# Batch 0's last stages on the PSUM pools of the dense layers, and batch 1's first matmuls ahead of the first dense matmul

## The chip, the cores and the metric

One Trainium2 chip, one core. The metric is the device time of one execution in microseconds (us), without tracing. Every kernel here was run several times on the same chip as the kernel before, alternating with it; a profiled execution was taken beside those.

## The reference

A global filter (real FFT over 3008 positions, product with a learnt filter, inverse FFT) is followed by a two-layer network with an exact gelu:

```python
X = np.fft.rfft(x, axis=1)                      # x: 8 x 3008 x 256
y = np.fft.irfft(X * (filt_r + 1j * filt_i)[None], n=x.shape[1], axis=1)
h = y.reshape(8 * 3008, 256) @ w_in             # 256 x 2048
g = 0.5 * h * (1.0 + erf(h / np.sqrt(2.0)))
out = g @ w_out                                 # 2048 x 256, float32
```

## The kernel before

In this text an evacuation is the copy of a finished PSUM bank (where TensorE writes) into SBUF, a store goes from SBUF to DRAM, and a readback fetches what was stored.

Each transform is a two-stage DFT, 3008 = 47 x 64, written as matmuls with tables T1 to T4 that the kernel makes for itself. The program order is written by hand; a scheduler does not reorder it.

**The front** handles batch 0 alone. Its stages c1, c1t (transposes), c2 (with the filter product), c3, c3t (transposes) and c4 pass everything through SBUF, while the tables are made beside them:

```python
def dup_filters(self, eng, k0, k):           # filter rows 0..63 copied to rows 64..127
    for k in range(k0, k0 + k, 2):
        o, i = (self.F[r:r + 64, :, k:k + 2, :].rearrange("p t a b -> p t (a b)") for r in (64, 0))
        eng.tensor_copy(out=o, in_=i)

def table_3_turn(self, q):                   # T3i from T3, with the sign columns turn_r, turn_i
    k = slice(8 * q, 8 * q + 8)
    for r in range(2):
        self.nc.vector.tensor_scalar(out=self.T3i[:, k, r, :], in0=self.T3[:, k, 1 - r, :],
                                     scalar1=self.turn[r], scalar2=None, op0=ALU.mult)

def c4(self, u, eng):                        # last stage of batch 0: y
    d = self.st[0, "d", u // 2]
    for half in range(2):
        ps = self.bank("ps_c4", "v")
        for i in range(4):
            self.nc.tensor.matmul(ps[:, 94 * i:94 * i + 94], lhsT=d[...], rhs=T4c, ...)
        self._evac(yv, ps[...], eng[half], 1.0 / self.S)
```

```python
m.load_x(1)                                  # batch 1's x, 8 loads on the GpSimd queue
m.load_w_out(0)                              # second-layer weights, 2 loads behind them
m.load_w_out(8)
...
wide = ctx.enter_context(ExitStack())
m.psum(wide, v=(4, 1), t=(4, 1))             # eight PSUM banks for c3t and c4
for u in range(10):
    if u < 8:
        m.c3t(u)
    if u >= 2:
        m.c4(u - 2, (act, False if u > 7 else act))
wide.close()
m.psum(ctx, h=(3, 1), o=(2, 1), f=(3, 1))    # the eight banks of the steady part
```

**The steady part** is a sequence of slots. A slot has two first-layer matmuls (`mm1`, 128x512, gelu on ScalarE from a bank "h") and, from slot 16 on, four second-layer matmuls of the tile before (`mm2`, into a bank "o"). The transforms of the later batches are laid into slots. These pass through DRAM: stage 1 stores `a`, which is read back as `b`; stage 3 stores `v`, which is read back as `d`. Stage 1:

```python
self.pa = pool("pa", 3)                      # three a buffers
...
def s1(self, b, c):                          # four groups c = 0..3 for each batch
    a = self.pa.tile([128, 2, 4, 256], BF16, tag="a", name="a_sb")
    ps = [[self.bank("ps_s1", "h" if i == h == 0 else "f") for h in range(2)] for i in range(2)]
    ...                                      # eight matmuls from x
    for i in range(2):
        for h in range(2):                   # four evacuations by VectorE
            self._evac(a[:, h, 2 * i:2 * i + 2, :]..., ps[i][h], False)
    for r in range(2):
        for h in range(2):                   # four stores of 96 KB on the sync queue
            nc.sync.dma_start(out=o[:, w:w + 4, :], in_=a[64 * r:64 * r + 48, h])
```

```python
# batch 1: first slot and spacing of stage 1, slot of b's readback, stage 2 ... stage 4
s1, n1, r1, s2, n2, r2, s4, n4 = 1, 4, 16, 26, 2.8, 61, 68, 0.72
...
for s in range((NT + 1) * 16):
    t, jc = s // 16, s % 16
    for f, a in at.pop(s, ()):               # the stages laid into this slot come first
        f(*a)
    if t >= 1:
        m.mm2(t - 1, jc)
    if t < NT:
        m.mm1(t, jc)
```

So stage 1 of batch 1 stands in slots 1, 5, 9 and 13.

## Time and profile before

| | |
|---|---|
| time | 772.72 us, median of 3 runs (772.1 to 775.15) |
| profiled execution | span 770.6 us |
| TensorE busy | 99% of the span |
| last c4 matmul starts | 37.82 us |
| second pair of first-layer matmuls starts | 39.84 us |
| first second-layer matmul starts | 49.13 us |

The page, the seam, the front and the stage-4 wait are shown in the prediction. How to read such lines: PE is TensorE, PEld its weight loads, DVE VectorE, ACT ScalarE, POOL GpSimd and SPq the sync queue. A timeline line has the start and the length in us, the engine, the line of the program, the operation, output and inputs by name and shape, and how many instructions the line joins. The square bracket is idle time of that engine before the line and what the profile thinks ended it. L296 (before) and L300 (after) are stage 1; L482 and L486 the first dense layer; L509 and L513 the second; L271 and L275 VectorE's evacuations; L459 and L463 are c4.

DMA issues between 38 and 50 us (what, queue, count, KB each, median us from issue to landing):

```profile
R<-a_sb SPq DMA_DIRECT2D x14, 96.0 KB, 2.3
```

A store of stage 1 takes 2.3 us there in the median. The four stores of the first group took 3.1 to 3.7 us.

### The profile page before, as it was taken

How to read it: one execution, taken by the hardware profiler on the slowest of the kernel's cores; microseconds unless marked ns; L12 is line 12 of the kernel's file. 1: busy time of each engine (PE TensorE's matmuls, PEld its weight loads, DVE VectorE, ACT ScalarE, POOL GpSimd, SP SyncE). 2: the span in 40 equal slices, each digit the busy share in tenths (PEclk: the TensorE clock that was granted, in tenths of full speed). 3: DMA queues.
4: the chain of work that ended last, by engine and by line, in shares of the span. 5: the costliest groups of instructions: out<-in, count | busy, mean ns of one | idle time of the engine just before them, and what ended most of it. 6: DMA issues, size and time to landing. Idle time of an engine off the chain costs nothing.

```text
span 770.6 us, 15044 instructions
## 1 busy us (share of the span) xinstructions
PE 763.5 (99%) x6057; PEld 527.5 (68%) x6057; DVE 398.5 (52%) x737; ACT 566.7 (74%) x977; POOL 62.5 (8%) x154
## 2 busy tenths in 40 slices
PE   8999999999999999999999999999999999999998
PEld 5857666776766766677777777667676777766666
DVE  8957755564545645466463664627646366411011
ACT  6879855897568975699656996579865798666663
POOL 7701100010000200011000110001100000000000
PEclk9999999999999999999999999999999999999999
DMA  9884645366163661636526364345553422410111
GB/s 153 150 197 115 136 125 129 115 138 155 40 173 88 128 158 47 187 79 125 138 58 176 85 133 124 83 151 105 114 137 84 136 83 70 123 42 28 42 42 55
DMA packets 87270, 85.66 MB, mean 111 GB/s; under 512 B 6688, under 2 KB 77472, under 8 KB 87200
## 3 DMA queue, kind: packets, MB, share of 16 engines
q1 hardware_dynamic: 78816, 68.70, 31.3%
q0 software_dynamic: 8384, 16.00, 14.1%
q8 instruction: 47, 0.77, 0.4%
q14 instruction: 23, 0.19, 0.1%
HBM read 54.00 MB, written 46.66 MB: 131 GB/s over the span
## 4 chain that ended last, share of the span: by engine, by line
PE 94%; DMA 3%; POOL 2%; issue 0%; DVE 0%; POOLq 0%; SPq 0%
PE ps_o L509 43%; PE ps_h L482 42%; PE ps_s L369 2%; PE ps_s L344 2%; PE ps_s L319 2%; PE ps_s L296 2%; DMA x_sb<-in_x_dram 2%; POOL x_sb L83 1%; DMA F<-in_filt_i_dram 1%; POOL F L97 1%; DMA d_sb<-R 0%; POOL F L92 0%; PE ps_e L499 0%; POOL T1s L282 0%; DVE ost L522 0%
## 5 line engine op out<-in xcount | busy, mean ns | idle before, releaser
L485 ACT ACTIVATE g_sb<-ps_h 128x512 bf16<-128x512 f32 x752 | 438.0, 597 | 183.4 <-PE ps_h L482 172.6
L509 PE MATMUL ps_o<-w_out_sb,g_sb 128*128 128x256 bf16 x2992 | 447.5, 273 | 0.0
L482 PE MATMUL ps_h<-y_sb,w_in_sb 128*128 128x512 bf16 (+3 forms) x1600 | 445.8, 366 | 0.7 <-DMA x_sb<-in_x_dram 0.7
L509 PEld LDWEIGHTS <-g_sb 128*128 128x128 bf16 x2992 | 283.9, 98 | 134.3 <-issue 9.9
L482 PEld LDWEIGHTS <-w_in_sb 128*128 128x128 bf16 x1600 | 154.7, 98 | 23.7 <-issue 1.1
L515 DVE COPY ost<-ps_o 128x512 f32<-128x512 f32 x93 | 63.8, 686 | 143.5 <-PE ps_o L509 143.4
L327 DVE TENSOR_TENSOR p<-ps_s,F 128x512 bf16<-128x512 f32 x84 | 58.1, 692 | 105.8 <-ACT p L326 89.4
L273 DVE TENSOR_SCALAR y_sb<-ps_s 128x376 bf16<-128x376 f32 x112 | 61.0, 548 | 80.7 <-PE ps_s L369 80.7
L271 DVE CAST a_sb<-ps_s 128x512 bf16<-128x512 f32 x112 | 69.4, 683 | 27.7 <-PE ps_s L296 27.7
L271 DVE CAST v_sb<-ps_s 128x512 bf16<-128x512 f32 x84 | 57.4, 685 | 2.9 <-PE ps_s L344 2.9
L325 ACT ACTIVATE p<-ps_s 64x512 bf16<-64x512 f32 x84 | 49.8, 593 | 2.0
L326 ACT CAST p<-ps_s 64x512 bf16<-64x512 f32 x84 | 48.5, 577 | 1.0
L369 PEld LDWEIGHTS <-d_sb 96*128 96x128 bf16 x448 | 30.7, 97 | 25.6 <-DMA d_sb<-R 0.6
L102 POOL COPY gate<-p 1x1 bf16<-1x1 bf16 x48 | 8.5, 176 | 470.7 <-DVE p L329 470.7
L329 DVE TENSOR_TENSOR p<-p 128x512 bf16<-128x512 bf16 x84 | 35.7, 425 | 2.9
L369 PE MATMUL ps_s<-T,d_sb 96*128 96x94 bf16 x448 | 36.3, 204 | 0.1
L328 DVE TENSOR_TENSOR p<-p,F 128x512 bf16<-128x512 bf16 x84 | 34.9, 415 | 0.0
L83 POOL DMA_DIRECT2D x_sb<-in_x_dram x64 | 32.6, 511 | 13.3 <-issue 12.8
L344 PE MATMUL ps_s<-p,T 128*128 128x256 bf16 x168 | 32.1, 273 | 0.0
L319 PE MATMUL ps_s<-b_sb,T 128*128 128x256 bf16 x168 | 32.1, 273 | 0.0
L344 PEld LDWEIGHTS <-T 128*128 128x128 bf16 x168 | 16.4, 98 | 20.1 <-DVE p L329 0.5
L319 PEld LDWEIGHTS <-T 128*128 128x128 bf16 x168 | 16.4, 98 | 13.4
(113 smaller groups left out, 195.0 us busy)
## 6 DMA issues: line engine op xcount, KB each, us to landing
out_dram<-ost SPq DMA_DIRECT2D x93, 256.0 KB, 2.4
x_sb<-in_x_dram POOLq DMA_DIRECT2D x64, 188.0 KB, 3.6
R<-a_sb SPq DMA_DIRECT2D x112, 96.0 KB, 2.1
b_sb<-R SPq DMA_DIRECT2D x28, 384.0 KB, 4.1
R<-v_sb SPq DMA_DIRECT2D x42, 256.0 KB, 3.3
d_sb<-R SPq DMA_DIRECT2D x56, 192.0 KB, 4.7
w_in_sb<-in_moe_w_in_dram POOLq DMA_DIRECT2D x2, 512.0 KB, 9.0
w_out_sb<-in_moe_w_out_dram POOLq DMA_DIRECT2D x2, 512.0 KB, 11.0
```

Source lines behind the costliest of these rows:

```text
L271: self.nc.vector.tensor_copy(out=out, in_=in_)
L273: self.nc.vector.tensor_scalar(out=out, in0=in_, scalar1=scale, scalar2=None, op0=ALU.mult)
L319: nc.tensor.matmul(ps[:, 256 * i:256 * i + 256], lhsT=self.T2[:, k].rearrange("p a b -> p (a b)"), rhs=self.st[b, "b", k // 6][:, k % 6, : ...
L325: nc.scalar.activation(out=p2[0:64], in_=ps[64:128], func=AF.Copy, scale=-1.0)
L326: nc.scalar.copy(out=p2[64:128], in_=ps[0:64])
L327: nc.vector.tensor_tensor(out=p1, in0=ps, in1=f(0), op=ALU.mult)
L344: nc.tensor.matmul(ps[:, 256 * i:256 * i + 256], lhsT=self.T3[:, k].rearrange("p a b -> p (a b)"), rhs=w[:, 256 * i:256 * i + 256], start= ...
L369: nc.tensor.matmul(ps[:, 94 * i:94 * i + 94], lhsT=d[:, (grp % 2) * 4 + i, 128 * half:128 * half + 128], rhs=t4, start=True, stop=True)
L482: nc.tensor.matmul(ps[:, o:o + n], lhsT=self.w_in_sb[:, dc, jc * 128:jc * 128 + 128], rhs=self.ring[:, dc, off:off + n], start=(dc == 0), ...
L485: nc.scalar.activation(out=self.st["g", t][:, jc, :], in_=ps, func=AF.Gelu)
L509: nc.tensor.matmul(ps[:, tile_i % 2, :], lhsT=g[:, jc, tile_i * 128:tile_i * 128 + 128], rhs=self.w_out_sb[:, jc, :], start=(jc == 0), sto ...
L515: nc.vector.tensor_copy(out=ost, in_=ps)
```

## The change

The intent: VectorE's small table work early in the kernel is shortened (sign columns by memsets, one filter copy to ScalarE, other small work later), and the seam between batch 0's transform and the dense layers is closed. For that c3t and c4 use the banks of the steady part, so no pool is closed and reopened, and batch 1's first stage-1 group moves in front of the first dense matmul. The core of the diff, with cuts:

```diff
 def dup_filters(self, eng, k0, k):
-            eng.tensor_copy(out=o, in_=i)
+            (eng.copy if eng is self.nc.scalar else eng.tensor_copy)(out=o, in_=i)
 ...
-    def turn_signs(self, g):      # five VectorE operations on 128x1 columns
-        ts(out=q, in0=self.p, scalar1=64.0, scalar2=-64.0, op0=ALU.is_ge, op1=ALU.mult)
-        ...
+    def signs(self, g):           # eight memsets
+        for t, s in zip(self.turn, (-1.0, 1.0)):
+            set_(t, s)
+            for lo in (32, 96):
+                set_(t[lo:lo + 32], -s)
+        set_(self.wtc, 2.0)
+        set_(self.wtc[0:4], 1.0)
 ...                               # weights_4: VectorE -> GpSimd, after the w_out loads
 ...                               # table_2_rows earlier, T1c later
+    m.dup_filters(nc.scalar, 0, 2)
     m.table_3_copy(1, False)
-    m.dup_filters(nc.vector, 0, 4)
+    m.dup_filters(nc.vector, 2, 2)
 ...
-        ps = self.bank("ps_c3t", "t", BF16)
+        ps = self.bank("ps_c3t", "f", BF16)
 ...
-            ps = self.bank("ps_c4", "v")
+            ps = self.bank("ps_c4", "h" if (2 * u + half) % 5 < 3 else "o")
 ...
-    wide = ctx.enter_context(ExitStack())
-    m.psum(wide, v=(4, 1), t=(4, 1))
+    m.psum(ctx, h=(3, 1), o=(2, 1), f=(3, 1))
     for u in range(10):
         if u < 8:
             m.c3t(u)
         if u >= 2:
-            m.c4(u - 2, (act, False if u > 7 else act))
-    wide.close()
-    m.psum(ctx, h=(3, 1), o=(2, 1), f=(3, 1))
+            m.c4(u - 2, (False if u > 7 else act, act))
 ...
-            s1, n1, r1, s2, n2, r2, s4, n4 = 1, 4, 16, 26, 2.8, 61, 68, 0.72
+            s1, n1, r1, s2, n2, r2, s4, n4 = 0, 4, 15, 25, 2.8, 61, 68, 0.72
```

Stage 1 of batch 1 now stands in slots 0, 4, 8 and 12.

More of the change, by code (lines that the diff above doesn't have):

```diff
@@ L137, in table_1 @@
         ts(out=hc, in0=h, scalar1=-2.0 * PI, scalar2=2.0 * PI, op0=ALU.mult, op1=ALU.add)
-        self.turn_signs(g)
-        self.weights_4(g)
+        self.table_2_rows(g)
         w, r = g.tile([128, 2, K1], FP32, name="w1"), g.tile([128, 2, K1], FP32, name="r1")
@@ L177, in table_2_angle @@
                                    in1=jn.unsqueeze(1).to_broadcast([128, 6, NB]), op0=ALU.mult, op1=ALU.add)
+            self.T1c = g.tile([2 * NA, 96], BF16, name="T1c")
+            v.tensor_copy(out=self.T1c.rearrange("p (k h r) -> p k h r", h=2, r=2),
+                          in_=self.T1.rearrange("p (h r k) -> p k h r", h=2, r=2))
             ts(out=w[:, 6:12], in0=w[:, 0:6], scalar1=n6, scalar2=None, op0=ALU.add)
@@ L183, in table_2_angle, with weights_4 @@
            op0=ALU.logical_shift_left)
-    def turn_signs(self, g):
-        ts = self.nc.vector.tensor_scalar
-        q, b = (g.tile([128, 1], FP32, name=n) for n in ("q64", "b32"))
+    def signs(self, g):
+        set_ = self.nc.vector.memset
         self.turn = [g.tile([128, 1], FP32, name=n) for n in ("turn_r", "turn_i")]
-        ts(out=q, in0=self.p, scalar1=64.0, scalar2=-64.0, op0=ALU.is_ge, op1=ALU.mult)
-        self.nc.vector.tensor_tensor(out=q, in0=self.p, in1=q, op=ALU.add)
-        ts(out=b, in0=q, scalar1=32.0, scalar2=2.0, op0=ALU.is_ge, op1=ALU.mult)
-        ts(out=self.turn[0], in0=b, scalar1=1.0, scalar2=-1.0, op0=ALU.mult, op1=ALU.add)
-        ts(out=self.turn[1], in0=b, scalar1=-1.0, scalar2=1.0, op0=ALU.mult, op1=ALU.add)
+        for t, s in zip(self.turn, (-1.0, 1.0)):
+            set_(t, s)
+            for lo in (32, 96):
+                set_(t[lo:lo + 32], -s)
+        self.wtc = g.tile([128, 1], FP32, name="wtc")
+        set_(self.wtc, 2.0)
+        set_(self.wtc[0:4], 1.0)
+    def weights_4(self, g):
+        ts = self.nc.gpsimd.tensor_scalar
+        q, self.wt = (g.tile([128, 1], FP32, name=n) for n in ("q48", "wt"))
+        ts(out=q, in0=self.p, scalar1=48.0, scalar2=-48.0, op0=ALU.is_ge, op1=ALU.mult)
+        self.nc.gpsimd.tensor_tensor(out=q, in0=self.p, in1=q, op=ALU.add)
+        ts(out=self.wt, in0=q, scalar1=2.0, scalar2=1.0, op0=ALU.is_ge, op1=ALU.add)
     def unit_matrices(self, g, cols):
@@ L218, in table_2_swap @@
                        "act", 1.0 - 2.0 * i)
-    def weights_4(self, g):
-        ts = self.nc.vector.tensor_scalar
-        q, self.wt, self.wtc = (g.tile([128, 1], FP32, name=n) for n in ("q48", "wt", "wtc"))
-        ts(out=q, in0=self.p, scalar1=48.0, scalar2=-48.0, op0=ALU.is_ge, op1=ALU.mult)
-        self.nc.vector.tensor_tensor(out=q, in0=self.p, in1=q, op=ALU.add)
-        ts(out=self.wt, in0=q, scalar1=2.0, scalar2=1.0, op0=ALU.is_ge, op1=ALU.add)
-        ts(out=self.wtc, in0=self.p, scalar1=4.0, scalar2=1.0, op0=ALU.is_ge, op1=ALU.add)
     def table_4(self, t4, t1, wt, tag, eng):
@@ L562 @@
     m.warm_up(10)
+    m.signs(g)
     m.table_1(g)
-    m.table_2_rows(g)
-    m.T1c = g.tile([2 * NA, 96], BF16, name="T1c")
-    nc.vector.tensor_copy(out=m.T1c.rearrange("p (k h r) -> p k h r", h=2, r=2),
-                          in_=m.T1.rearrange("p (h r k) -> p k h r", h=2, r=2))
     m.gen = m.py.tile([128, 2, K1, NB], FP32, tag="y", name="gen")
@@ L637 @@
     m.load_w_out(8)
+    m.weights_4(g)
     warm = g.tile([128, 1], FP32, name="warm")
```

## The prediction

> **What bounds the kernel now.** I read the page first, for the shares and the chain that ended last.
>
> ```profile
> PE 763.5 (99%) x6057; PEld 527.5 (68%) x6057; DVE 398.5 (52%) x737; ACT 566.7 (74%) x977; POOL 62.5 (8%) x154
> PE ps_o L509 43%; PE ps_h L482 42%; PE ps_s L369 2%; PE ps_s L344 2%; PE ps_s L319 2%; PE ps_s L296 2%; DMA x_sb<-in_x_dram 2%; POOL x_sb L83 1%; DMA F<-in_filt_i_dram 1%; POOL F L97 1%; DMA d_sb<-R 0%; POOL F L92 0%; PE ps_e L499 0%; POOL T1s L282 0%; DVE ost L522 0%
> ```
>
> TensorE is busy for 99% of the span, and 85% of the chain is the two dense layers (L482, L509). So time can come only from two places: an earlier first dense matmul, or a hole in the TensorE stream later. The seam between batch 0's transform and the dense layers, in the timeline (start, duration, what; in brackets the idle time before it):
>
> ```profile
> 37.28 0.55 DVE L273 TENSOR_SCALAR y_sb<-ps_c 128x376 bf16<-128x376 f32 x1
> 38.06 0.55 DVE L273 TENSOR_SCALAR y_sb<-ps_c 128x376 bf16<-128x376 f32 x1 [0.22 <-PE ps_c L459]
> ...
> 38.76 0.59 PE L482 MATMUL ps_h<-y_sb,w_in_sb 128*128 128x512 bf16 x2 [0.73 <-DMA x_sb<-in_x_dram]
> 39.28 0.63 PE L296 MATMUL ps_s<-x_sb,T1s 47*64 47x512 bf16 x8
> 39.84 1.90 PE L482 MATMUL ps_h<-y_sb,w_in_sb 128*128 128x512 bf16 x8
> 41.66 1.06 PE L296 MATMUL ps_s<-x_sb,T1s 47*64 47x512 bf16 x8
> ```
>
> TensorE idles 0.73 us before its first dense matmul. The profile names an x load; the program's waits there are on VectorE, ScalarE and the weights (landed by 26.0), and the last evacuation of y ends at 38.06+0.55 = 38.61. That is the true releaser. Right after, 8 matmuls of batch 1 (L296), which need nothing of batch 0's y, take TensorE from 39.19 (one 0.22 us matmul after the second dense one began) to 39.84: 0.65 us that would have fitted in the hole.
>
> From 49 us on I compared start-to-start intervals of TensorE matmuls with the median of the same pair. One excess counts, 459 ns against 216, at 99.5:
>
> ```profile
> 99.96 0.36 PEld L369 LDWEIGHTS <-d_sb 96*128 96x128 bf16 x8 [0.57 <-DMA d_sb<-R]
> ```
>
> The first stage-4 matmul of batch 1 waits for its operand to come back from DRAM: 0.24 us.
>
> The front, in the timelines of VectorE and GpSimd:
>
> ```profile
> 13.99 0.90 DVE L97 COPY F<-F 64x1024 bf16<-64x1024 bf16 x2
> 14.92 0.76 DVE L271 COPY b_sb<-ps_c1t 128x512 bf16<-128x512 bf16 x2
> 15.82 1.23 DVE L412 TENSOR_TENSOR p<-ps_c,F 128x1024 bf16<-128x1024 f32 x1
> ...
> 17.48 2.35 DVE L412 TENSOR_TENSOR p<-ps_c,F 128x1024 bf16<-128x1024 f32 x2
> ```
>
> ```profile
> 17.41 1.05 POOL L97 COPY F<-F 64x1024 bf16<-64x1024 bf16 x1 [0.55 <-DMA F<-in_filt_i_dram]
> ```
>
> VectorE works without a break from 13.99 to 30.08 (the filter products, 1.14 us each). Before that, the four groups of stage-1 matmuls start at 5.89, 8.61, 10.57 and 12.45, each 0.10 to 0.11 us after an x transfer landed (5.79, 8.50, 10.46, 12.35 in the trace's DMA records). The front is paced by loads.
>
> **What the Trainium skill says.** "PSUM — Partial Sum Buffer", Engine vs sequencer instructions: TensorE may pull a weight load ahead, but matmuls start and complete in program order. The trace agrees: the L296 matmuls, whose x had landed at 31.6 and 32.5, stood behind the dense ones until 39.28. So moving them in the program is what fills the hole. "TensorE: Matmul & The Clock Gate", Phases on the wall clock: 512 columns take about 216 ns back to back; the trace's median is 216. "ScalarE: Activation LUTs", What ACT_TABLE_LOAD costs: an activation costs 186 ns + 0.833 ns per element, so 1.04 us for 1024; the trace has 1.02 for a 128x1024 one. I use 1.0 us for the filter copy that moves to ScalarE, an estimate.
>
> **The change, part by part.** Stripped of line numbers, the instruction orders of both kernels differ little.
>
> 1. Sign columns: nine tiny VectorE operations between 1.86 and 3.06 go (six for signs and the T4c weight, three for T4's weight, which reappear on GpSimd after its loads); six memsets come in, about 0.05 us apart by the two memsets at 1.35 and 1.39. The tables of angles are ready some 0.8 us sooner. Worth 0: the first stage-1 matmul waits for ten warm-ups (1.46 to 5.91) and for x (5.79), the next for x at 8.50. Nothing of GpSimd's load issues moves.
>
> 2. One of two filter copies goes from VectorE (0.45 us) to ScalarE. The next VectorE instruction, the b evacuation, needs transposes that start at 14.01 and take 0.61, so it can begin at 14.65, not 14.92: 0.27 gained. But product 2 (at 17.48+1.13 = 18.61) needs the first GpSimd copy, which starts when a filter lands and ends at 17.41+1.05 = 18.46. With about 0.05 for the semaphore it starts near 18.5, and the rest follow. Gain at the end of the products: 0.1 us. ScalarE has 1.0 us more, finishes its b evacuation near 16.8 instead of 16.14, needed at about 18.1: no wait.
>
> 3. c3t moves from four banks to three. It waits for the evacuation three transposes back, and VectorE (0.69 us each) is behind by less: no new wait. c4 moves from four banks to five: no gain, since ScalarE's evacuations (14 in 5.48 us) already run back to back. But no pool is closed and reopened, so banks of f and h are free before y ends. In the last two groups VectorE now takes the first half and ScalarE the second. VectorE can then evacuate from 37.83 on without its 0.22 wait, ending at 38.38; ScalarE starts on the last half at 38.06 and ends at 38.54 (0.48 each). With the 0.1 of part 2: 38.28 and 38.44.
>
> 4. Stage 1 of batch 1 moves before the first dense matmul. Its eight matmuls follow c4's last (start 37.82), about 37.9 to 38.45, in the hole. The first dense matmul starts near 38.48, against 38.76: gain 0.28. The 0.65 us at 39.19 vanish: gain 0.65.
>
> 5. The second stage-1 group waits 0.42 us for VectorE's a evacuations (the gap inside the 41.66 line: 1.06 for 0.63). VectorE now starts them at 38.38-0.1, four dense slots before it starts at 38.48 + 1.83 = 40.3; the distance grows from 1.89 to 2.02, gain 0.13. The fourth group's 0.36 stays.
>
> 6. Batch 1's stages 2 and 3 come a slot (0.87 us) earlier, stage 4 stays at slot 68. The v stores end a slot earlier, so the 0.24 us wait at 99.5 goes: gain 0.24. Danger: the readback b lands at 56.45 for a need at 57.65 (slot 26). Stage 1 starts 39.28 - 37.93 = 1.35 us earlier and so do its stores, so b lands near 55.3 by estimate; slot 25 comes at about 55.9. It just fits.
>
> Sum: 0.28 + 0.65 + 0.13 + 0.24 = 1.30 us, carried through a TensorE stream without holes to the end: 772.72 - 1.30 = 771.4.
>
> **The rivals.** (a) A new wait at the seam: the stage-1 tile in h takes the bank of c4's twelfth evacuation (ScalarE, done near 37.5), and had the wait fallen on the last one, the group would end 0.6 us later and the gain would be 0.7 us. The order of banks speaks against it. (b) The moved stage-1 group makes VectorE the limit: 16 evacuations at 0.61 us are 9.8 us in a stretch where TensorE needs 9.2 us; VectorE's lag then eats part of item 4, and 0.9 us in all remains. (c) b lands late and slot 25 waits: up to 0.5 us lost, total gain 0.8. (d) The front gives its full 0.45, if GpSimd's first copy came earlier too: 1.6 us. Nothing moves that load, so unlikely. (e) The ScalarE copy delays the transposes' evacuation and stretches the front by up to 0.7; slack of 1.3 us speaks against.
>
> **Range and chances.** The theories lie between 0.6 and 1.7 us of gain; three runs of the kernel before spread over 3 us with a median that may be off by half a us. I give 770.0 to 772.9. Two per cent are 15.5 us; the whole front is 38.7 us and nearly all of it is kept, and no step could cost so much. So within 2% is nearly sure.
>
> **What would show it.** Right: the first L296 group (its new line) starts near 37.9, the first dense matmul near 38.5 with no idle above 0.1 before it; first second-layer matmul at 48.2 instead of 49.13; no excess at stage 4; product 2 on VectorE at 18.5; end of span 1.3 us sooner, as seen already at 101 us. Wrong: stage-1 groups still at 5.9 and 8.6 are required; if they start earlier the front was not paced by loads. A wait before stage 2 near 56 would confirm (c); a second stage-1 group over 1.0 us long, (b). If the time after 101 us moved differently from the time before, the cause lies where I looked for none.

## The result, and the profile after

The changed kernel is correct. It took 772.58 us (median of 6 runs, 771.83 to 773.58) against 772.76 us for the kernel before (6 runs, 772.1 to 775.15). The ratio is 0.9996 with a 95% interval of 0.998 to 1.0011: the same. Ratios here are the mean time of one kernel's runs over that of the other's runs of the same rounds, so not quite the ratio of the medians quoted. The time lies in the predicted range, but of the predicted gain of 1.30 us only about 0.3 us can be seen (0.0004 of 772.7), less than the interval. The range, 770.0 to 772.9, also holds the time of the kernel before. The rest of this document asks where the other microsecond went.

The profiled execution of after happened to be its slowest run (773.58, span 771.8). Its seam and the first slots, TensorE timeline:

```profile
38.28 1.45 PE L463 MATMUL ps_c<-T4c,d_sb 96*128 96x94 bf16 x24
39.66 0.63 PE L300 MATMUL ps_s<-x_sb,T1s 47*64 47x512 bf16 x8
40.22 1.90 PE L486 MATMUL ps_h<-y_sb,w_in_sb 128*128 128x512 bf16 x8
...
47.22 1.01 PE L300 MATMUL ps_s<-x_sb,T1s 47*64 47x512 bf16 x8
48.16 1.04 PE L486 MATMUL ps_h<-y_sb,w_in_sb 128*128 128x512 bf16 x4
49.54 1.02 PE L486 MATMUL ps_h<-y_sb,w_in_sb 128*128 128x512 bf16 x4 [0.34 <-DVE a_sb L275]
50.40 0.60 PE L513 MATMUL ps_o<-w_out_sb,g_sb 128*128 128x256 bf16 x4
```

Before has no hole between the fourth stage-1 group and the second layer:

```profile
46.88 1.01 PE L296 MATMUL ps_s<-x_sb,T1s 47*64 47x512 bf16 x8
47.83 1.47 PE L482 MATMUL ps_h<-y_sb,w_in_sb 128*128 128x512 bf16 x6
49.13 0.60 PE L509 MATMUL ps_o<-w_out_sb,g_sb 128*128 128x256 bf16 x4
```

Three things are to be seen. In after the seam is closed: stage 1 follows c4, the dense matmuls follow stage 1, and no line has a bracket. It all happens late, though: c4 ends at 39.7 where before's last c4 matmul started at 37.82. And there is a new hole of 0.34 us at 49.5, four dense matmuls after the fourth stage-1 group. (The bracket counts from the modelled end of a matmul; by the table below the hole cost TensorE 0.5 us.) VectorE's timeline around it:

```profile
45.28 2.48 DVE L275 CAST a_sb<-ps_s 128x512 bf16<-128x512 f32 x4 [0.28 <-PE ps_s L300]
48.79 1.29 DVE L275 CAST a_sb<-ps_s 128x512 bf16<-128x512 f32 x2 [1.03 <-PE ps_h L486]
```

The fourth group's matmuls began at 47.22, but VectorE evacuated it only from 48.79, after 1.03 us of idling. The profile names a dense matmul as the releaser, which these evacuations do not need. In the trace's DMA records the first group's four stores were issued from 42.03 to 43.50 and landed from 47.38 to 48.67, the last 0.12 us before VectorE went on. That is the releaser. In before they were issued from 41.70 and had landed by 46.23, before the fourth group's matmuls at 46.88. DMA issues of after in the same stretch:

```profile
R<-a_sb SPq DMA_DIRECT2D x12, 96.0 KB, 4.2
```

The same store now takes 4.2 us in the median instead of 2.3, and the first group's four took 5.2 to 5.4 us instead of 3.1 to 3.7.

The late end of the front has another cause. VectorE's timeline, then GpSimd's, of after:

```profile
16.04 1.23 DVE L416 TENSOR_TENSOR p<-ps_c,F 128x1024 bf16<-128x1024 f32 x1 [0.21 <-PE ps_c L412]
17.19 1.21 DVE L260 TENSOR_SCALAR T3i<-T,turn_r 128x512 bf16<-128x512 bf16 x1
18.32 1.12 DVE L260 TENSOR_SCALAR T3i<-T,turn_i 128x512 bf16<-128x512 bf16 x1
19.36 1.20 DVE L416 TENSOR_TENSOR p<-ps_c,F 128x1024 bf16<-128x1024 f32 x1
```

```profile
17.21 3.12 POOL L97 COPY F<-F 64x1024 bf16<-64x1024 bf16 x3 [0.16 <-POOL vt_sb L578]
```

The same two operations in before:

```profile
16.96 0.35 DVE L256 TENSOR_SCALAR T3i<-T,turn_r 128x512 bf16<-128x512 bf16 x1
17.22 0.35 DVE L256 TENSOR_SCALAR T3i<-T,turn_i 128x512 bf16<-128x512 bf16 x1
```

In after, the turns of T3i ran while GpSimd's filter copies ran, and took 1.21 and 1.12 us instead of 0.35; the second filter product (product 1 in the prediction's count, which starts at 0) then began at 19.36 instead of 17.48. The Trainium skill has this: "SBUF — State Buffer", Who interferes with whom, says that a VectorE copy, cast or tensor_scalar in a two-port mode uses a pair of ports that it shares with GpSimd, that whoever issues first holds it for the whole instruction, and that the other blocks. The trace agrees in the lengths: each long turn ends 0.15 us after a GpSimd copy would (3.12 / 3 = 1.04 us each, so near 18.25 and 19.29). Who came first cannot be read off it: the first turn's record starts at 17.19, the copy's at 17.21.

So there were two suspects: the a buffers with their stores, and the ports. They differ in kind. The front ends at another time in each profile, even for the same kernel, so I split each profile at c4's last matmul.

### The profile page after: what moved, and what is told of

It is laid out like the page before. It is cut to its first block, busy times and chain, and to the rows that moved or that the text cites. A ratio compares the mean times of both kernels' runs of the same rounds, so it can differ in the third digit from the quotient of the medians. Undisturbed runs are those within 1.5% of the kernel's fastest.

```text
span 771.8 us, 15047 instructions
## 1 busy us (share of the span) xinstructions
PE 763.0 (99%) x6057; PEld 527.2 (68%) x6057; DVE 399.0 (52%) x735; ACT 567.8 (74%) x978; POOL 63.7 (8%) x157
## 4 chain that ended last, share of the span: by engine, by line
PE 97%; DMA 1%; DVE 1%; POOL 0%; issue 0%; SPq 0%; DVEq 0%; POOLq 0%
PE ps_o L513 42%; PE ps_h L486 42%; PE ps_s L373 2%; PE ps_s L348 2%; PE ps_s L323 2%; PE ps_s L300 2%; DMA x_sb<-in_x_dram 1%; PE ps_c L434 1%; PE ps_c3t L449 0%; PE ps_c L412 0%; DMA d_sb<-R 0%; PE ps_warm L267 0%; POOL x_sb L83 0%; PE ps_c L463 0%; DVE T3i L260 0%; PE ps_c1t L399 0%
```

## The experiments

Twelve kernels were run, all correct, five rounds each. This table has one profiled execution of each. The columns: start of c4's last matmul; from it to the first second-layer matmul (the seam with slots 0 to 15); from that matmul to the gelu of slot 96; from c4's last matmul to the end of the span; and the time over that of before with its 95% interval. All but the last are single executions, in us. Only the intervals of the last four rows lie wholly below 1.

| kernel | c4 last | to 2nd layer | to slot 96 | c4 to end | ratio |
|---|---|---|---|---|---|
| before | 37.82 | 11.31 | 81.64 | 732.82 | |
| before, repeated (b_again) | 38.78 | 11.31 | 81.63 | 732.80 | 0.9999 [0.9985, 1.0013] |
| late_turn | 39.60 | 11.31 | 81.54 | 732.77 | 1.0009 [0.9996, 1.0021] |
| before_pa4 | 38.52 | 11.31 | 81.38 | 732.56 | 1.0006 [0.9993, 1.002] |
| before_wout_early | 38.21 | 11.31 | 81.44 | 732.61 | 0.999 [0.9975, 1.0005] |
| after | 39.53 | 10.87 | 81.52 | 732.25 | 0.9996 [0.998, 1.0011] |
| after, repeated (a_again) | 38.27 | 11.60 | 81.27 | 732.73 | 0.9997 [0.9985, 1.001] |
| early_turn | 38.30 | 11.38 | 81.24 | 732.47 | 0.9995 [0.9983, 1.0008] |
| seam_only | 37.60 | 12.14 | 81.23 | 733.24 | 0.9997 [0.9984, 1.0009] |
| turn_n5 | 37.51 | 9.71 | 82.73 | 732.30 | 0.9996 [0.9982, 1.0009] |
| after_pa4 | 37.84 | 10.37 | 81.34 | 731.68 | 0.9983 [0.9971, 0.9996] |
| turn_pa4 | 37.55 | 10.37 | 81.54 | 731.76 | 0.9985 [0.9972, 0.9997] |
| wout_early | 38.49 | 10.37 | 81.82 | 732.05 | 0.9987 [0.9974, 0.9999] |
| turn_wout_early | 37.55 | 10.37 | 81.27 | 731.49 | 0.9981 [0.9968, 0.9993] |

### First lot: is it the ports?

These four ran on one chip; before took 773.35 us there.

**a_again**: the changed kernel once more, unaltered.

> The changed kernel unaltered, for a second draw of its front. Theory A (port collision): whether VectorE's two turn copies of table 3 that start near 17 us overlap a GpSimd filter copy depends on load jitter; in the traced execution of after they took 1.21 and 1.12 us in place of 0.35, and the products were 1.7 us late. If they collide again, the span is 771 to 772 us; if not, the turns take 0.35 us, product 1 starts near 17.6 and the span is about 770. Theory B (systematic later loads): turns are 0.35 us or long, but the last filter loads again land after 22.5 us and set the start of the dense layers. Ratio to before 0.998 to 1.000 either way. The 0.5 us hole in the dense stream near 48 us should be there again.

Measured: 773.05 us. The ports did not collide (first turn 0.34 us), and c4's last matmul came at 38.27. The hole was larger, and here the profile named it rightly. TensorE, VectorE, and the view of waits from 38 to 60 us (us in total, times, longest):

```profile
46.90 1.04 PE L486 MATMUL ps_h<-y_sb,w_in_sb 128*128 128x512 bf16 x4
49.01 1.02 PE L486 MATMUL ps_h<-y_sb,w_in_sb 128*128 128x512 bf16 x3 [1.07 <-DVE a_sb L275]
```

```profile
48.27 1.89 DVE L275 CAST a_sb<-ps_s 128x512 bf16<-128x512 f32 x3 [1.76 <-DMA R<-a_sb]
```

```profile
DVE a_sb L275 <- DMA R<-a_sb: 1.8, 1, 1.8
PE ps_h L486 <- DVE a_sb L275: 1.1, 1, 1.1
```

The first group's stores had landed at 48.15, and VectorE went on at 48.27, the same 0.12 us later as in after. The chain is: stores late, a buffer not free, VectorE waits, the group's tile keeps one of the three h banks, the dense layer finds no bank. What after won at the seam (from c4's last matmul to the second dense pair 1.14 us, 2.02 before) it lost here, and 11.60 is more than before's 11.31.

**b_again**: the kernel before once more, unaltered.

> The kernel before against itself: the noise floor. Ratio 1.000 within 0.001. Turn copies at 17 us: 0.35 us where they begin before GpSimd's first filter copy, over 1 us where not. Last filter load lands at 21.2 us in the trace of before; if it lands near 23 us here too, the later loads of the traced after are jitter and not the change.

Measured: 773.36 us. Its second turn collided too, at 17.40 for 1.13 us, with a GpSimd copy that started at 17.28, and c4's last matmul came at 38.78 instead of 37.82. The collision is not a property of the change.

**early_turn**: the changed kernel with T3's copy ahead of the filter copy on ScalarE, and the turns ahead of the first filter product.

```diff
     m.table_3(1)
-    m.dup_filters(nc.scalar, 0, 2)
     m.table_3_copy(1, False)
+    m.dup_filters(nc.scalar, 0, 2)
 ...
-    m.c2(0)
     m.table_3_turn(1)
+    m.c2(0)
```

> The changed kernel with the table-3 copy on ScalarE in front of the filter copy, and the two turn copies in front of the first filter product, so that they end near 16.4 us, before GpSimd copies anything. Theory A: both take 0.35 us, product 1 starts near 17.5, the seam gain shows, span 769.5 to 770.5, ratio to before about 0.9975. Theory B: no change against after unless loads are early.

Measured: 772.81 us. The turns took 0.34 and 0.46 us, at 15.98 and 16.24, clear of GpSimd. The time did not fall, and the hole was there (0.85 us, up to 48.81).

**late_turn**: the kernel before with the turns one product later, so that they must collide.

```diff
     m.c2(0)
-    m.table_3_turn(1)
     m.warm_up(1)
     m.c2(1)
+    m.table_3_turn(1)
```

> The kernel before with the turn copies moved behind product 1, where GpSimd surely copies. Theory A: each takes about 1.0 to 1.2 us in place of 0.35, the products after it come 1.4 to 1.8 us later, and the time is 1.3 to 1.8 us more than before (ratio 1.0017 to 1.0023). Theory B: the time stays within 0.5 us of before.

Measured: 774.15 us, turns of 1.02 and 1.12 us, ratio 1.0009. This meets neither expectation. A collision of both turns costs between nothing and 1.6 us by the interval. The ports are real (the turns grew from 0.35 to over 1 us), but removing the collision in the changed kernel gained nothing that can be seen, so they are not where the microsecond went.

### Second lot: the a buffers

Before took 772.64 us here. These ask whether the hole holds the missing gain.

**after_pa4**: the changed kernel with a fourth a buffer; a v buffer is given up for the room.

```diff
-        self.pa = pool("pa", 3)
+        self.pa = pool("pa", 4)
-        self.pv = pool("pv", 3)
+        self.pv = pool("pv", 2)
```

> The changed kernel with four a buffers in place of three (and two v buffers in place of three to make room). Theory C: the hole of 0.5 to 1.2 us near 48 us is the fourth stage-1 group waiting for an a buffer, whose stores stand behind the w_out load; with a fourth buffer it is gone, from the first dense matmul to the first second-layer matmul it takes 9.7 us in place of 10.2 to 10.9, and the time falls by 0.5 to 1.0 us against the changed kernel (ratio to before 0.998 to 0.999). Rival D: the hole is TensorE waiting for loads that are late in themselves (w_out, x); then it stays or moves to the first second-layer matmul, and the time stays at 0.9997. A new wait of up to 0.5 us at stage 2 near 57 us is possible, since the readback b lands no earlier.

Measured: 771.30 us, ratio 0.9983, which is 1.3 us less than before. TensorE's timeline, the same stretch as above:

```profile
45.54 1.01 PE L300 MATMUL ps_s<-x_sb,T1s 47*64 47x512 bf16 x8
46.48 1.90 PE L486 MATMUL ps_h<-y_sb,w_in_sb 128*128 128x512 bf16 x7
48.21 0.60 PE L513 MATMUL ps_o<-w_out_sb,g_sb 128*128 128x256 bf16 x4
```

The dense matmuls run through, and the second layer starts at 48.21 (one of eight records is missing in the middle line). The stores are as slow as ever, 5.1 us in the median; nothing waits for them now.

**turn_pa4**: early_turn with the same two pools.

> Early turns and four a buffers together. Theories A and C both: no turn over 0.5 us, no hole at 48 us, first second-layer matmul near 48.7 us, ratio to before 0.998. If only one of the two is right, 0.9985 to 0.9995.

Measured: 771.56 us, ratio 0.9985. With the hole gone, taking the turns from GpSimd's way still adds nothing that can be told from after_pa4.

**turn_n5**: early_turn with three a buffers, stage 1 in slots 0, 5, 10 and 15, and the readback in slot 16.

```diff
-            s1, n1, r1, s2, n2, r2, s4, n4 = 0, 4, 15, 25, 2.8, 61, 68, 0.72
+            s1, n1, r1, s2, n2, r2, s4, n4 = 0, 5, 16, 25, 2.8, 61, 68, 0.72
```

> Early turns, and the four stage-1 groups five slots apart (0, 5, 10, 15) with the readback issued a slot later; no more buffers. Theory C: the fourth group now comes when its buffer's stores have landed, no hole at 48 us, 9.8 us from first dense to first second-layer matmul, ratio to before about 0.9985; stage 2 may wait up to 0.5 us for b near 57 us, which would show that the stores' bandwidth and not their start sets b. Rival D: hole of the same size somewhere before 52 us.

Measured: 772.25 us, ratio 0.9996. The first 16 slots ran best of all (9.71 us: five slots apart, all four groups take 0.63 us on TensorE, where at four slots the second and fourth take 1.01 because VectorE has not freed their banks), and the time came back as a wait of stage 2 for the readback, in the waits from 38 to 60 us:

```profile
PEld L323 <- DMA b_sb<-R: 1.7, 1, 1.7
```

Both columns together are 9.71 + 82.73 = 92.44 us, within 0.2 of early_turn's 11.38 + 81.24 = 92.62. Spreading stage 1 only moves the wait.

**seam_only**: the kernel before with the new banks, the swapped halves and the new slots alone; the front as before.

```diff
-        ps = self.bank("ps_c3t", "t", BF16)
+        ps = self.bank("ps_c3t", "f", BF16)
 ...                                   # the c4 banks, the pools and the slots as in the change
-            s1, n1, r1, s2, n2, r2, s4, n4 = 1, 4, 16, 26, 2.8, 61, 68, 0.72
+            s1, n1, r1, s2, n2, r2, s4, n4 = 0, 4, 15, 25, 2.8, 61, 68, 0.72
```

> The kernel before with the seam of the change alone (pools, halves, stage 1 first, slots 15 and 25); tables, sign columns and filter copies as before. Theory C: the same hole near 48 us as in the changed kernel, so the ratio to before is 0.9985 to 1.000; first dense to first second-layer matmul 10.2 to 10.9 us. If the changed tables at the front cost something by themselves (x and filters landing 0.2 to 1 us later in three traces of each), this one shows filters landing near 21.2 us and is faster than the changed kernel by up to 1 us.

Measured: 772.50 us, ratio 0.9997, as the whole change. So the signs and the filter copy are worth nothing that can be measured. after_pa4 ran in the same rounds, and its slowest run (771.86) is faster than the fastest run of seam_only (771.99), which has three a buffers. The profile of seam_only has the largest hole; the waits from 38 to 60 us:

```profile
DVE a_sb L271 <- DMA R<-a_sb: 2.3, 1, 2.3
PE ps_h L482 <- DVE a_sb L271: 1.6, 1, 1.6
```

### Third lot: why are the stores slow?

Before took 772.47 us for the first three. Theory: the stores share the DMA engines with the w_out load, which is still under way when they are issued.

**before_pa4**: the control for the pools, the kernel before with four a buffers and two v buffers.

> Control: the kernel before with four a buffers and two v buffers. Theory C: before has no hole at its fourth stage-1 group, which comes later against its buffer's stores, so the buffers alone are worth nothing: ratio 1.000 within 0.001. If it is 0.9985 instead, the gain of the fourth buffer has nothing to do with the change.

Measured: 773.18 us, ratio 1.0006. The pools by themselves gain nothing. Whether two v buffers cost something lies within the interval.

**wout_early**: the changed kernel with three a buffers, and the w_out load issued some 12 us sooner, among GpSimd's filter copies.

```diff
-    m.dup_filters(nc.gpsimd, 4, 20)
+    m.dup_filters(nc.gpsimd, 4, 8)
+    m.load_w_out(0)
+    m.load_w_out(8)
+    m.dup_filters(nc.gpsimd, 14, 10)
 ...
+            if q == 2:
+                m.dup_filters(nc.scalar, 12, 2)
 ...
     m.load_x(1)
-    m.load_w_out(0)
-    m.load_w_out(8)
```

> The changed kernel, three a buffers, with the w_out load issued by GpSimd after its fourth filter copy, behind w_in, so that it fills the idle DMA stretch near 26 to 30 us (the copy for k = 12, 13 moves to ScalarE to make room). Theory C (the stores stand behind w_out): the first a stores land 2 to 3 us after issue and not 5 to 6, no hole at 48 us, b lands near 55 us, no wait at stage 2; gain of the change comes out, ratio to before 0.998 to 0.9985, if the front is not delayed by more than 0.5 us. Rival E (any three-buffer rotation stalls with stage 1 this early): the hole stays at 0.5 us or more.

Measured: 771.77 us, ratio 0.9987. GpSimd's timeline shows the load, and the DMA issues from 38 to 50 us the stores:

```profile
22.22 1.79 POOL L116 DMA_DIRECT2D w_out_sb<-in_moe_w_out_dram  x2
```

```profile
R<-a_sb SPq DMA_DIRECT2D x15, 96.0 KB, 2.2
```

w_out landed at 30.81 and 33.21 (44.56 and 48.15 in after), the stores took 2.2 us, and TensorE had no hole. The first group's stores landed by 44.72, before the fourth group's matmuls at 46.18, so three buffers were enough. The loads of batch 1's x had stayed where they were (the last landed at 42.04), so they are not what slows the stores. In the seven kernels with the change and the late load, the last of the first group's four stores landed close to the second w_out load, from 0.18 us before it (seam_only) to 0.52 us after it (after). This fits the Trainium skill, "DMA: Bandwidth & Descriptors", Queues, rings and completion order, which says that each DMA engine "round-robins between the queue rows it has work for, at *packet* granularity". With w_out under way the stores got through, at half the pace or less. The trace shows the two durations; it does not show single packets taking turns.

**turn_wout_early**: early_turn with the same early load.

> The same with the early turns, so free of port collisions at 17 us. Expected the fastest of all: ratio 0.9975 to 0.9985, and a smaller spread of times (under 1 us between lowest and highest). If the early turns are worth nothing on average it equals wout_early.

Measured: 771.33 us (770.82 to 771.79), ratio 0.9981. By median and ratio it is level with after_pa4 (771.30, 0.9983) as the best of all; the two intervals overlap almost wholly. It does it without another buffer.

**before_wout_early**: the control for it, the kernel before with the early load. Before took 773.31 us in its rounds.

> Control for the two early-w_out kernels: the kernel before with the w_out load issued among the filter copies (and one filter copy on ScalarE for room), all else as before. Theory C (the load only hurts where stage 1 comes a slot earlier and needs the a buffer back at once): the kernel before had no wait for an a buffer, so the early load gains nothing here: ratio 1.000, within 0.0012; the first a stores land within 2 to 2.5 us of issue; second dense pair to first second-layer matmul 9.3 us as before. Rival (the early load is worth about 1 us by itself, for instance because the stores and the x load have the DMA engines to themselves): ratio 0.9985 to 0.999, and the whole of the gain of the early-w_out kernels would not be the change's.

Measured: 772.63 us, ratio 0.999 [0.9975, 1.0005]. By time this is inconclusive: 0.999 lies within both expectations, and before's nine runs include two of 774.85 and 775.11. In the profile, the stretch at issue did not move at all: 11.31 us to the second layer, as in every form of before, with stores of 2.1 us instead of 2.3. From c4 to the end it has 732.61, between before_pa4 (732.56) and before (732.82). So behind the seam the early load shows no gain beyond the 0.2 us by which the forms of before differ without it; what it may do to the front is open.

It supports one thing that the prediction had only argued. Here the profile names another releaser of the first dense matmul of before:

```profile
39.15 0.59 PE L482 MATMUL ps_h<-y_sb,w_in_sb 128*128 128x512 bf16 x2 [0.73 <-DVE y_sb L273]
```

The idle time is the same 0.73 us that was put down to an x load in before: it fits VectorE's last evacuation of y, which ended 0.15 us before that matmul in both (38.61 and 39.00).

## Why the prediction was right and wrong

**What bounds the kernel: right.** The gain could come only from the seam and from later holes. The kernels that did reach it gained in the seam and lost no time to the new hole.

**Item 1 (sign columns, worth 0): right.** The stage-1 groups of after start at 6.19, 9.05, 10.91 and 12.80, each 0.13 to 0.14 us after its x landed (6.06, 8.91, 10.78, 12.67), as required. seam_only without this part is as fast. There are eight memsets, not six, and "about 0.05 us apart" was too short (they start from 1.35 to 2.11, 0.76 / 7 = 0.11 us apart); it did not matter.

**Item 2 (filter copy, 0.1 us): not resolved, and something was missing.** Product 2 started at 20.49 in after instead of the foreseen 18.5, since product 1 had come at 19.36. I had looked at when GpSimd's copies end, and not at what VectorE runs beside them. The collision comes and goes with the landing of the x and filter loads, in before as well; late filters alone do harm too (in a_again, without a collision, product 2 waited until 19.21 for a GpSimd copy whose filter landed at 17.99). Together they move c4's last matmul by a microsecond between executions. The copy itself took ScalarE 1.04 us, as estimated from the Trainium skill ("ScalarE: Activation LUTs", What ACT_TABLE_LOAD costs) for 1024 elements. The mean cost of the collision stays open: late_turn 1.0009 [0.9996, 1.0021], and no gain from turn_pa4 over after_pa4.

**Items 3 and 4 (banks, halves and the moved group): right.** Predicted 0.28 + 0.65 = 0.93 us, 0.1 of it the front's (item 2); from c4's last matmul to the second dense pair after has 1.14 and before 2.02, so 0.88. Rival (a), a wait of the moved group for a late bank, did not come.

**Item 5: the step that failed.** The prediction says "The fourth group's 0.36 stays", and sums up a gain "carried through a TensorE stream without holes to the end". The fourth group's gap inside its eight matmuls did stay (1.01 for 0.63). But the stream got a hole two slots behind it. I had followed the group to its PSUM banks and to VectorE, and not its output buffer to the landing of the stores, which is what frees it. With three a buffers, group 4 waits for group 1's stores. In before these had landed 0.65 us before the group's first matmul (46.23 against 46.88) and 1.12 us before VectorE began to evacuate it (47.35). The change moved the stores earlier relative to the w_out load: the first was issued 9.5 us after the load in before (41.70 against 32.23), and 8.0 and 7.6 us after it in after and a_again (42.03 against 34.01, 40.78 against 33.21). So more of the load runs beside them, and they became slower by more than they were issued sooner. By its bracket the hole was 0.34, 1.07, 0.85 and 1.61 us in the four profiles with three buffers and the late load (spacing 4), and absent in all four kernels that removed its cause in either way. That it fluctuates fits a race between loads. The size of the missing term can be read off the table: to the second layer, 10.87, 11.60, 11.38 and 12.14 with it and 10.37 without, on average 1.1 us. That is most of the gain. The predicted 0.13 for the second group was also too large: without the hole the stretch from the second dense pair to the second layer is 9.23 us against 9.29, so 0.06. The seam and this stretch together thus have 0.95 of the predicted 1.06.

**Item 6 (stage-4 wait, 0.24 us): not shown, and a smaller wait was overlooked.** The wait is not simply gone; in after, from 94 to 103 us:

```profile
PEld L373 <- DMA d_sb<-R: 0.6, 1, 0.6
```

A slot (0.87 us) was to be gained, but against the gelu of slot 68 the last v store moved by 0.4 us only (94.44 against 102.53, before 93.72 against 101.38): an output store (93.24) and VectorE's evacuation for it now stand in front, and v landed at 97.29. By start-to-start intervals, as in the prediction, the wait cost TensorE 0.24, 0.23, 0.15, 0.00 and 0.05 us in the five forms of before, and 0.00 to 0.57 in the nine of the change (0.28 in after, 0.57 in wout_early, which is much of why its 732.05 is behind the others' 731.5 to 731.8). The means are 0.13 and 0.12: it comes and goes in both. What all five forms of before have and none of the nine has is another wait, of the last stage-3 group for VectorE's filter product. It cost 0.14 us, against the prediction's "One excess counts". In before:

```profile
92.54 0.11 PEld L344 LDWEIGHTS <-T 128*128 128x128 bf16 x2 [0.47 <-DVE p L329]
```

In after the same bracket is 0.19, and costs nothing. Taking these waits and those for b off the stretch to slot 96 leaves 81.23 to 81.26 us in all fourteen profiles, so nothing else of that size changed in it. Why the change ended the stage-3 wait was not tested.

**The rivals.** (b), VectorE as the limit with 0.9 us left of the gain, was nearest in place and wrong in mechanism: VectorE did hold up the dense layer, but it idled itself for up to 2.3 us before that (seam_only), for a buffer. (c), a late b, was right and hidden: while the hole delayed the slots, b came in time; with the hole gone turn_pa4 shows 0.6 us of it and after_pa4 0.2, and turn_n5 1.7 (idle time before the weight load; TensorE lost 0.29, nothing and 1.39). (d) and (e) did not show.

**The sum.** From c4's last matmul to the end, before has 732.77 to 732.82 with its pools and loads unaltered. The prediction asked for about 1.2 to 1.3 less, 731.5 to 731.6 (0.1 of it may be the front's). after, a_again and early_turn have 732.25, 732.73 and 732.47, on average 0.3 less than before, which is what the timed runs say; seam_only, whose profile drew the largest hole, has 733.24. The kernels without the hole have 731.49, 731.68, 731.76 and 732.05, and their timed gains are 1.0 to 1.5 us. The best of them shows where a gain of the predicted size came from: 0.88 at the seam, 0.06 at the second group, 0.14 at stage 3 and 0.21 at stage 4, the last by the luck of that execution. Behind slot 96 all fourteen profiles agree within 0.12 us. So the seam was priced rightly, and a buffer ate it. That the time of after lay in the range says little for the prediction, since the range held a gain of nothing as well.

**What stays open.** The mean cost of the port collision; whether the second v buffer that was given up costs something (1.0006, within noise); and how much of the 1.0 to 1.5 us of the early-load kernels is the early load's own in the front, since its control could not be told from either expectation by time.

## What to carry to other kernels

Before moving work earlier into a hole, follow its output buffer to its release, not only its inputs and banks. A rotation of three buffers that was just long enough can fall short when the stores that free it slide under a bulk load. Put bulk loads where the DMA engines have time, and when a microsecond matters, take several profiles of each kernel and split them at a point behind the jitter: here the front moved by 1 us between executions of one kernel, while the distance from c4 to the end held within 0.05 us for before (three profiles with its pools and loads unaltered).

## What the Trainium skill lacked or had wrong

- **How far a store is held up by another queue's load.** "DMA: Bandwidth & Descriptors" gives the turn-taking between queues but no cost. Here 96 KB stores on the sync queue took 2.1 to 2.3 us in the median without the w_out load of the GpSimd queue beside them (before_wout_early, wout_early) or with its end only (before), and 4.2 to 5.3 us with the w_out load under way (after, a_again, after_pa4, seam_only). The first group's stores alone took 2.0 to 2.3 us in wout_early, 3.1 to 3.7 in before and 5.2 to 5.4 in after.
- **How blocked ports look in a profile.** "SBUF — State Buffer" is right on the blocking, and speaks of engines measured as slower, but does not say how a wait for the ports shows in a profile: here not as idle time but as the instruction's own length, 1.02 to 1.21 us for a 128x512 bf16 tensor_scalar of 0.34. Nothing in the profile names GpSimd; only laying the two timelines together does.
- **A releaser can be misnamed.** No page that I used says it: the same 0.73 us wait was put down to an x load in before and to VectorE's evacuation in before_wout_early, and after's wait for stores to a dense matmul.
